# Nine-token loads, k^T v in array quarters, and weights staged in f32 and cast an expert ahead, in a fused linear-attention and top-1 MoE kernel

## The chip, the cores and the metric

The kernel runs on one core of a Trainium2 chip. The metric is device time in microseconds of one launch; three runs are taken, and their median counts. A profile of one execution by the hardware profiler is shown beside them.

## What is computed

Linear attention for 8 batches and 8 heads of 576 tokens and 64 dimensions, a root-mean-square norm of each head's output, and then a mixture of 8 experts that sends each of the 4608 tokens (512 wide, the 8 heads side by side) to one expert:

```python
kv = np.einsum('bhsd,bhse->bhde', k, v)
out = np.einsum('bhsd,bhde->bhse', q, kv)
rms = np.sqrt(np.mean(out * out, axis=-1, keepdims=True) + 1e-06)
x = (out / rms * g_norm)            # -> (4608, 512)
logits = x @ w_gate                 # (512, 8)
expert_idx = np.argmax(logits, axis=1)
gate_w = softmax(logits)[chosen]
for e in range(8):
    xe = x[expert_idx == e]
    ye = np.maximum(xe @ w1[e], 0.0) @ w2[e]   # w1 512 x 1024, w2 1024 x 512
    out[expert_idx == e] = gate_w * ye
```

All inputs and the output are f32. With the inputs of this case the experts get 564, 494, 600, 572, 539, 654, 585 and 600 tokens.

## The kernel before

The work has two stages. Every engine's instruction order is written out by hand.

**Attention, 36 slots.** Two batches make a group of nine slots; a slot is 128 tokens. `load_qkv` (L157) brings 512 tokens of all heads of one batch, four tokens a partition (runs of 1 KB), and `load_rem` (L164, DMAs at L167) the last 64 tokens of each head in 64-partition transfers with 256 B runs, the two batches of a group side by side. All of these go out on SP's queue; six `ld` buffers hold k, v and q of two batches, and the loads of batch b+2 are issued two slots ahead of batch b+1 (L415), so that they wait for buffers.

For each batch, `kv_mm` (L200, matmul L216) forms k^T v for one pair of heads: the two heads of the pair go to the two column halves of TensorE; four matmuls each have 128 rows, a fifth has 64. `kv_copy` (L221), `kv_t` (L227) and `kv_gate` (L235) put the result into `kvs`, 144 columns a head pair: 128 for the two heads on a block diagonal, 16 for the router's logits.

For each slot, `heads` (L192) has POOL copy the queries into contiguous form (L197), four slots at a time; `x_qt` (L251) transposes them on TensorE, `x_qs` (L263) copies the result on ScalarE, and `x_mm` (L267, matmul L278) multiplies with `kvs`: four matmuls, or eight of 64 weight columns in the ninth slot of a group. `x_norm` (L284) squares (ACT, L294), sums (DVE, L299), takes the inverse root on ACT (L303, L305) and scales (DVE, L307 and L311) into f16 rows `xg`.

After nine slots a `Route` (L318) finds each token's expert and its rank there, and `send` (L375) scatters the nine slots' rows into `xs_scratch` in device memory by nine indirect DMAs on POOL's queue (L386). Eight DMAs of zero rows (`blank`, L443) on SP's queue fill the rows below the capacity of 640 before anything is scattered. The lists `mid`, `late` and `last` hang the work of the next batches and the routes onto slots.

**FFN, nine jobs.** Experts 0 to 6, then a job "left" of up to 128 rows for what exceeds an expert's 640 rows, then expert 7. A job's rows come transposed by `fetch` (L562, DMA L567 on SP). `one` (L581) makes 320 columns of the first product in four matmuls (hp, L589), with the relu on ACT (L596); `two` (L600) makes 128 rows of the second (yp, L603), DVE scales by the gate weight (L608) and POOL scatters the rows to the output (L611). The left-over job gathers its rows by POOL (L544) and transposes them on TensorE (L630).

**Weights** (L119). w1 goes as f32 into one staging buffer on SP's queue (L125), and four casts with the norm's gain make the f16 copy (L132), by POOL for the first two experts and by DVE inside the FFN, two jobs ahead. w2 is cast in the DMA itself, on POOL's queue (L138). Each has three f16 buffers.

Of the kernel before, what the change touches and what calls it, by code (L numbers as in the profile page):

```python
# [28 lines left out]
def kernel(  # L29
# [16 lines left out]
    E = 8  # L46
# [3 lines left out]
    CAP = CT * 128  # L50
    NOV = (N - CAP) // 128
# [19 lines left out]
    o = 144 + CT  # L71
    for P in range(4):
        for bb in range(2):
            for j in range(4):
                c32[:, o + 9 * P + 4 * bb + j] = (2 * P + bb) * S + 4 * ar + j
        c32[:64, o + 9 * P + 8] = 2 * P * S + 512 + ar[:64]
        c32[64:, o + 9 * P + 8] = (2 * P + 1) * S + 512 + ar[:64]
# [40 lines left out]

    class Weights:  # L119
        def __init__(self, e):  # L120
            self.e = e if isinstance(e, bass.DynSlice) else slice(e, e + 1)

        def stage(self):
            self.st = P_w.tile([128, 4, F], F32, tag="wst", bufs=1, name="wst")
            nc.sync.dma_start(  # L125
                self.st, moe_w1[self.e, :, :].rearrange("o (t p) f -> p (o t) f", p=128)
            )

        def scale(self, eng, kk):
            if kk == 0:  # L130
                self.w1 = P_w.tile([128, 4, F], F16, tag="w1e", bufs=3, name="w1e")
            eng.tensor_scalar(  # L132
                self.w1[:, kk, :], self.st[:, kk, :], g2, 1.0, op0=ALU.mult, op1=ALU.mult
            )

        def second(self):
            self.w2 = P_w.tile([128, 8, D], F16, tag="w2e", bufs=3, name="w2e")
            nc.gpsimd.dma_start(  # L138
                self.w2, moe_w2[self.e, :, :].rearrange("o (t p) d -> p (o t) d", p=128)
            )  # L140
# [4 lines left out]
    W = [Weights(e) if e != "left" else None for e in order]  # L145

    with (
# [9 lines left out]
        def load_qkv(src, b):  # L157
            t = PA.tile([128, 8, 256], F32, tag="ld", bufs=6, name="ld")
            nc.sync.dma_start(
                t, src[b, :, 0:512, :].rearrange("h (p j) d -> p h (j d)", j=4)  # L160
            )
            return t

        def load_rem(src, b0, tag):  # L164
            t = PA.tile([128, 8, 64], F32, tag=tag, bufs=2, name=tag)
            for bb in range(2):
                nc.sync.dma_start(  # L167
                    t[64 * bb:64 * bb + 64, :, :],
                    src[b0 + bb, :, 512:576, :].transpose([1, 0, 2]),
                )  # L170
            return t

        ld, rem, qp, kvst = {}, {}, {}, {}

        def load_batch(b):
            ld["k", b] = load_qkv(k, b)
            ld["v", b] = load_qkv(v, b)
            if b % 2 == 0:
                rem["k", b // 2] = load_rem(k, b, "kr")
                rem["v", b // 2] = load_rem(v, b, "vr")  # L180
            if b == 0:
                nc.sync.dma_start(cf, c_f32.ap())
                nc.sync.dma_start(wg, moe_w_gate.rearrange("(t p) j -> p t j", p=128))
                nc.sync.dma_start(g2[0:64, :], g_norm.unsqueeze(1))
                nc.sync.dma_start(g2[64:128, :], g_norm.unsqueeze(1))
            ld["q", b] = load_qkv(q, b)
            if b % 2 == 0:
                rem["q", b // 2] = load_rem(q, b, "qr")
            if b == 0:
                nc.sync.dma_start(ch, c_f16.ap())  # L190

        def heads(b, j):  # L192

            if j == 0:
                qp[b] = PA.tile([128, 4, 8, 64], F32, tag="qp", bufs=2, name="qp")
            tv = ld["q", b].rearrange("p h (j d) -> p h j d", j=4)
            nc.gpsimd.tensor_copy(qp[b][:, j, :, :], tv[:, :, j, :])  # L197


        def kv_mm(b, i):  # L200
            if i == 0:
                kvst[b] = PSA.tile([128, 4, 64], F32, tag="kvp", bufs=1, name="kvp")
            kvp = kvst[b]
            kb, vb = ld["k", b], ld["v", b]
            kr, vr = rem["k", b // 2], rem["v", b // 2]
            r0 = 64 * (b % 2)
            for j in range(5):
                for hh in range(2):
                    h = 2 * i + hh
                    if j < 4:  # L210
                        lhs = kb[:, h, 64 * j:64 * j + 64]
                        rhs = vb[:, h, 64 * j:64 * j + 64]
                    else:
                        lhs = kr[r0:r0 + 64, h, :]
                        rhs = vr[r0:r0 + 64, h, :]
                    nc.tensor.matmul(  # L216
                        kvp[64 * hh:64 * hh + 64, i, :], lhs, rhs,
                        start=(j == 0), stop=(j == 4),
                    )

        def kv_copy(b):  # L221
            kvp, kvs = kvst[b], kvs_bufs[b % 4]
            for hh in range(2):
                ps = slice(64 * hh, 64 * hh + 64)
                nc.vector.tensor_copy(kvs[ps, :, 64 * hh:64 * hh + 64], kvp[ps, :, :])

        def kv_t(b):  # L227
            kvs = kvs_bufs[b % 4]
            kvtp = PSA.tile([128, 4, 128], F32, tag="misc", bufs=1, name="kvtp")
            for i in range(4):  # L230
                nc.tensor.transpose(kvtp[:, i, :], kvs[:, i, 0:128], ident)
            kvst[b] = PA.tile([128, 4, 128], F32, tag="kvt", bufs=1, name="kvt")
            nc.scalar.copy(kvst[b], kvtp)

        def kv_gate(b):  # L235
            kgp = PSA.tile([128, 4, 16], F32, tag="misc", bufs=1, name="kgp")
# [13 lines left out]

        def x_qt(s):  # L251
            P, r, b = split(s)
            if r < 8:
                j = r % 4
                src = qp[b][:, j, :, :]
            else:
                src = rem["q", P]
            qtp = PSA.tile([128, 4, 128], F32, tag="qtp", bufs=2, name="qtp")
            for i in range(4):
                nc.tensor.transpose(qtp[:, i, :], src[:, 2 * i:2 * i + 2, :], ident)  # L260
# [6 lines left out]
        def x_mm(s):  # L267
            P, r, b = split(s)
            if r < 8:
                parts = [(slice(0, 128), kvs_bufs[b % 4])]  # L270
            else:
                parts = [(slice(0, 64), kvs_bufs[(2 * P) % 4]),
                         (slice(64, 128), kvs_bufs[(2 * P + 1) % 4])]
            op = PSA.tile([128, 2, 512], F32, tag="op", bufs=2, name="op")
            for i in range(4):
                c0 = (i % 2) * 144
                for c, kvs in parts:
                    nc.tensor.matmul(  # L278
                        op[c, i // 2, c0:c0 + 144], qts[s][:, i, c], kvs[:, i, :],
                        start=True, stop=True,  # L280
                    )
# [36 lines left out]
        class Route:  # L318
# [28 lines left out]
            def ranks(self):  # L347

                G, oh = self.G, self.oh
                self.pp = PSA.tile([128, G, 8], F32, tag="misc", bufs=1, name="pp")  # L350
# [51 lines left out]
        for b in range(1, B):  # L402
            f = first_slot[b]
            n = 4 if b % 2 else 5
            plan = [[0, 1], [2, 3]] if n == 4 else [[0], [1, 2], [3]]
# [6 lines left out]
            for j in range(4):  # L412
# [322 lines left out]
```

## Time and profile before

| | |
|---|---|
| runs | 347.36 us median of 3 (342.71 to 352.43) |
| profiled execution | 340.94 us, of which the profile's span is 339.1 |
| attention | 0 to 177.35 us: PE busy 116.48, transfer share 0.89, 251 GB/s |
| FFN to the last yp | 177.35 to 332.80 us: PE busy 146.65, transfer share 0.89, 214 GB/s |
| tail | last rows scaled at 332.85, end of span 339.1 |
| busy in the span | PE 263.1, DVE 145.3, ACT 121.9, POOL 118.2 us |
| mean granted TensorE clock | 0.907 |

How to read it: the profile gives each engine's busy time, in total and in 40 slices of the span; the chain of waits follows the work that ended last back through whatever released it; the timeline lists the instructions of an engine in runs of equal ones, with the idle time before them in brackets and what ended it; windows give the same for chosen stretches, with the granted clock, the busy share of the 16 transfer engines and the rate. "issue" is time in which the profile shows nothing that an engine waited for. SPq and POOLq are the queues on which transfers are issued.

### The profile page before, as it was taken

The numbers are of one execution on the slowest core, as the hardware profiler recorded it, in microseconds if no ns is written. First come the engines' busy times: TensorE is split into PE (matmuls) and PEld (weight loads), VectorE is DVE, ScalarE is ACT, GpSimd is POOL, SyncE is SP. The second block draws the span as 40 slices with busy tenths as digits, with TensorE's granted clock in tenths as the row PEclk, the third lists the DMA queues.
The fourth block names the chain that finished last, engine by engine and source line by source line (L and its number), as shares of the span: only waits on it lengthen the run. The fifth ranks groups of instructions, "written<-read, shape, count | busy, mean of one in ns | idle before, by whom it ended". The sixth has DMA issues, their size and how long they took to land.

```text
span 339.1 us, 5512 instructions
## 1 busy us (share of the span) xinstructions
PE 263.1 (78%) x2119; PEld 187.4 (55%) x2119; DVE 145.3 (43%) x349; ACT 121.9 (36%) x295; POOL 118.2 (35%) x139
## 2 busy tenths in 40 slices
PE   0679499739986798753304999999999999779992
PEld 0578487628875677652202656464747474545650
DVE  0014516814674348578871253343340707054021
ACT  1024526234544354433201607070807070521620
POOL 4022020474117940758420052424250516225123
PEclk9999879987999599969555999999999999979998
DMA  7999999998699989547719978999999995999012
GB/s 237 222 324 305 269 274 350 244 359 286 190 279 342 367 272 226 130 100 151 278 48 181 292 204 154 279 172 265 287 221 327 175 346 158 270 256 223 24 53 95
DMA packets 84683, 78.30 MB, mean 231 GB/s; under 512 B 41771, under 2 KB 75819, under 8 KB 84656
## 3 DMA queue, kind: packets, MB, share of 16 engines
q1 hardware_dynamic: 70240, 54.29, 57.2%
q0 software_dynamic: 14416, 23.65, 30.0%
q8 instruction: 17, 0.28, 0.4%
q14 instruction: 10, 0.08, 0.1%
HBM read 66.46 MB, written 17.09 MB: 246 GB/s over the span
## 4 chain that ended last, share of the span: by engine, by line
PE 29%; DMA 24%; issue 20%; DVE 12%; POOL 6%; SPq 3%; ACT 3%; POOLq 1%; another core or an unknown queue 1%; DVEq 0%
DMA out_dram<-ys,idx 10%; PE op L278 9%; PE yp L603 5%; PE hp L589 5%; DMA xo<-xs_scratch,gi 4%; PE kvp L216 4%; POOL out_dram L611 4%; DMA ld<-in_v_dram 3%; DMA xs_scratch<-blank 3%; PE qtp L260 3%; SPq L167 2%; DMA ld<-in_q_dram 2%; DVE xg L311 2%; DVE dl L332 2%; PE kgp L238 1%
## 5 line engine op out<-in xcount | busy, mean ns | idle before, releaser
L596 ACT ACTIVATE ht<-hp 128x320 f16<-128x320 f32 (+1 forms) x136 | 57.9, 428 | 98.3 <-PE hp L589 62.6
L589 PE MATMUL hp<-xt,w1e 128*128 128x320 f16 (+1 forms) x544 | 76.9, 304 | 11.7 <-DMA xt<-xs_scratch 11.7
L611 POOL DMA_INDIRECT out_dram<-ys,idx x41 | 42.2, 1029 | 112.3 <-DVE ys L608 99.4
L589 PEld LDWEIGHTS <-w1e 128*128 128x128 f16 x544 | 53.3, 100 | 34.8 <-issue 11.8
L603 PE MATMUL yp<-w2e,ht 128*128 128x512 f16 x328 | 72.3, 379 | 0.0
L608 DVE TENSOR_SCALAR ys<-yp,mt 128x512 f32<-128x512 f32 x40 | 29.8, 750 | 91.6 <-PE yp L603 48.5
L278 PE MATMUL op<-kvs,qts 128*128 128x144 f32 (+1 forms) x320 | 51.3, 329 | 8.1 <-issue 5.2
L603 PEld LDWEIGHTS <-ht 128*128 128x128 f16 x328 | 32.1, 98 | 37.3
L386 POOL DMA_INDIRECT xs_scratch<-xg,sli x36 | 35.2, 979 | 50.0 <-DVE sli L384 39.4
L278 PEld LDWEIGHTS op<-kvs,qts 128*128 128x128 f32 (+1 forms) x320 | 43.2, 205 | 11.1 <-issue 6.0
L216 PE MATMUL kvp<-ld 128*64 128x64 f32 x512 | 25.3, 250 | 15.5 <-DMA ld<-in_v_dram 15.5
L197 POOL COPY qp<-ld 128x512 f32<-128x512 f32 x32 | 18.3, 614 | 53.3 <-DMA ld<-in_q_dram 53.2
L294 ACT ACTIVATE sq<-op 128x512 f32<-128x512 f32 x36 | 21.5, 597 | 41.3 <-PE op L278 30.2
L299 DVE TENSOR_REDUCE ms<-sq 128x8 f32<-128x512 f32 x36 | 24.5, 682 | 25.2 <-ACT sq L294 24.1
L265 ACT COPY qts<-qtp 128x512 f32<-128x512 f32 x36 | 21.0, 583 | 35.0 <-PE qtp L260 23.5
L216 PEld LDWEIGHTS kvp<-ld 128*64 128x64 f32 x512 | 20.6, 158 | 20.0 <-issue 19.0
L260 PE MATMUL qtp<-cf,qp 128*128 128x128 f32 x128 | 23.5, 315 | 8.8 <-issue 7.2
L311 DVE TENSOR_TENSOR xg<-op,rinv 128x512 f16<-128x512 f32 x36 | 24.5, 681 | 0.2
L260 PEld LDWEIGHTS qtp<-cf,qp 128*128 128x128 f32 x128 | 18.7, 169 | 9.5 <-issue 7.7
L132 DVE TENSOR_SCALAR w1e<-wst,g 128x1024 f16<-128x1024 f32 x28 | 21.0, 808 | 0.1
L307 DVE TENSOR_TENSOR lr<-op,rinv 128x64 f32<-128x64 f32 x36 | 8.1, 224 | 26.0 <-ACT rinv L305 19.4
L303 ACT ACTIVATE lnt<-ms,epsb 128x8 f32<-128x8 f32 x36 | 10.9, 302 | 11.0 <-DVE ms L299 8.9
(89 smaller groups left out, 143.5 us busy)
## 6 DMA issues: line engine op xcount, KB each, us to landing
wst<-in_moe_w_dram SPq DMA_DIRECT2D x9, 2048.0 KB
w2e<-in_moe_w_dram POOLq DMA_DIRECT2D x9, 1024.0 KB
ld<-in_k_dram SPq DMA_DIRECT2D x8, 1024.0 KB
ld<-in_v_dram SPq DMA_DIRECT2D x8, 1024.0 KB
ld<-in_q_dram SPq DMA_DIRECT2D x8, 1024.0 KB
xs_scratch<-blank SPq DMA_DIRECT2D x8, 193.5 KB
kr<-in_k_dram SPq DMA_DIRECT2D x8, 128.0 KB
vr<-in_v_dram SPq DMA_DIRECT2D x8, 128.0 KB
```

The costliest lines, as they stand in the source:

```text
L216: nc.tensor.matmul(kvp[64 * hh:64 * hh + 64, i, :], lhs, rhs, start=(j == 0), stop=(j == 4),)
L260: nc.tensor.transpose(qtp[:, i, :], src[:, 2 * i:2 * i + 2, :], ident)
L278: nc.tensor.matmul(op[c, i // 2, c0:c0 + 144], qts[s][:, i, c], kvs[:, i, :], start=True, stop=True,)
L294: nc.scalar.activation(sq.rearrange("p (c i h) n -> p c i (h n)", c=2, i=2), oc[:, :, :, 0:128], ACTF.Square,)
L299: nc.vector.reduce_sum(ms, sq, axis=AXX)
L311: nc.vector.tensor_tensor(xg[:, r, 0:512].rearrange("p (c i h n) -> p c i h n", c=2, i=2, h=2), ox, _bc(r4, 4, 64), op=ALU.mult,)
L386: nc.gpsimd.indirect_dma_start(out=xs_views[9 * self.P + g0 + t], out_offset=IndirectOffsetOnAxis(ap=sli[:, t:t + 1], axis=0), in_=xgs[sel ...
L589: nc.tensor.matmul(hp, self.w.w1[:, kk, f * 128:(f + 1) * 128], self.xt[:, kk, ws * wd:(ws + 1) * wd], start=(kk == 0), stop=(kk == 3),)
L596: nc.scalar.activation(self.ht[:, f, ws * wd:(ws + 1) * wd], hp, ACTF.Relu)
L603: nc.tensor.matmul(yp, self.ht[:, f, t * 128:(t + 1) * 128], self.w.w2[:, f, :], start=(f == 0), stop=(f == 7),)
L608: nc.vector.tensor_scalar(ys, yp, self.mt[:, t, 1:2].bitcast(F32), None, op0=ALU.mult)
L611: nc.gpsimd.indirect_dma_start(out=self.views[t], out_offset=IndirectOffsetOnAxis(ap=self.idx[:, t:t + 1], axis=0), in_=ys, in_offset=None ...
```

## The change

- **Loads.** k, v and q of a batch come in one form: 9 tokens of a head a partition, two heads on the 128 partitions, four head pairs along the row (runs of 2304 B). The remainder loads go. k and v have six buffers, q three of its own; the first batch's k and v come in two pieces each. The constants and the zero rows are issued by ACT.
- **k^T v.** A head's tokens now lie on one half of the partitions. For two head pairs, nine steps of four 64x64 matmuls: row half by head of the pair, column half by pair, accumulated apart for the two row halves.
- **Queries.** `x_qp` copies them slot by slot on POOL, four slots ahead. Every slot is two tokens of 64 partitions, and `x_mm` has eight matmuls of 64 weight columns in every slot. kvtp, kgp, pp and cp share the two PSUM buffers of qtp.
- **Capacity** 608 instead of 640: hp is 304 columns wide, the last of five yp tiles has 96 rows.
- **Weights.** Both are loaded as f32 on SP's queue into five staging buffers. w1 comes in four DMAs of 64 partitions (its rows ordered as x is now laid out), and is cast by DVE (POOL for the first expert), one expert ahead; w2 is cast by four ACT copies, one expert ahead. Two f16 buffers each. Expert 0's w1 and w2 and expert 1's w1 are loaded during attention.

```diff
-    CAP = CT * 128
+    CAP = 608
+    WIDTHS = [128, 128, 128, 128, 96]
...
-        def stage(self):
-            self.st = P_w.tile([128, 4, F], F32, tag="wst", bufs=1, name="wst")
+        def load1(self, buf):
+            self.s1 = buf.rearrange("p (t f) -> p t f", t=4)
+            view = moe_w1[self.e, :, :].rearrange("o (c i h p) f -> (o i) p c h f", c=2, i=2, h=2)
+            for i in range(2):
+                ps = slice(64 * i, 64 * i + 64)
+                for c in range(2):
+                    nc.sync.dma_start(self.s1[ps, 2 * c:2 * c + 2, :], view[i, :, c, :, :])
+
+        def load2(self, buf):
+            self.s2 = buf.rearrange("p (t d) -> p t d", t=8)
             nc.sync.dma_start(
-                self.st, moe_w1[self.e, :, :].rearrange("o (t p) f -> p (o t) f", p=128)
+                self.s2, moe_w2[self.e, :, :].rearrange("o (t p) d -> p (o t) d", p=128)
             )
...
-        def second(self):
-            self.w2 = P_w.tile([128, 8, D], F16, tag="w2e", bufs=3, name="w2e")
-            nc.gpsimd.dma_start(
-                self.w2, moe_w2[self.e, :, :].rearrange("o (t p) d -> p (o t) d", p=128)
-            )
+        def cast2(self, kk):
+            nc.scalar.copy(self.w2[:, 2 * kk:2 * kk + 2, :], self.s2[:, 2 * kk:2 * kk + 2, :])
...
-        def load_qkv(src, b):
-            t = PA.tile([128, 8, 256], F32, tag="ld", bufs=6, name="ld")
-            nc.sync.dma_start(
-                t, src[b, :, 0:512, :].rearrange("h (p j) d -> p h (j d)", j=4)
+        def load(name, b, parts=1):
+            src = {"k": k, "v": v, "q": q}[name]
+            tag, bufs = ("lq", 3) if name == "q" else ("lkv", 6)
+            ld[name, b] = PA.tile([128, 4, 9 * Dh], F32, tag=tag, bufs=bufs, name=tag)
+            view = src[b].rearrange("(i hh) (p j) d -> (hh p) i (j d)", hh=2, j=9)
...
+            for j in range(9):
+                js = slice(Dh * j, Dh * j + Dh)
                 for hh in range(2):
+                    rs = slice(64 * hh, 64 * hh + 64)
+                    for ipar in range(2):
+                        i = 2 * ip + ipar
+                        nc.tensor.matmul(
+                            kvp[64 * ipar:64 * ipar + 64, hh, Dh * ip:Dh * ip + Dh],
+                            kb[rs, i, js], vb[rs, i, js],
+                            start=(j == 0), stop=(j == 8),
+                        )
...
+        def x_qp(s):
+            P, r, b = split(s)
+            qps[s] = PA.tile([128, 2, 4, 64], F32, tag="qp", bufs=4, name="qp")
+            if r < 8:
+                tv = ld["q", b].rearrange("p i (j d) -> p j i d", j=9)
+                nc.gpsimd.tensor_copy(qps[s], tv[:, 2 * (r % 4):2 * (r % 4) + 2, :, :])
...
+            for ip in range(2):
+                for hh in range(2):
+                    for tok in range(2):
+                        kvs = kvs_bufs[(b if r < 8 else 2 * P + tok) % 4]
+                        nc.tensor.matmul(
+                            op[64 * tok:64 * tok + 64, ip, 144 * hh:144 * hh + 144],
+                            qts[s][:, 2 * tok + ip, 64 * hh:64 * hh + 64],
+                            kvs[:, 2 * ip + hh, :],
+                            start=True, stop=True,
+                        )
...
-            nc.sync.dma_start(
-                xs.ap()[e * N + CAP - 192:e * N + CAP, :].rearrange("(p r) c -> p (r c)", r=2),
+            nc.scalar.dma_start(
+                xs.ap()[e * N + CAP - 160:e * N + CAP + 32, :].rearrange("(p r) c -> p (r c)", r=2),
                 blank,
             )
...
+            if s + 4 < 36:
+                x_qp(s + 4)
...
             jobs[0].fetch()
-            W[1].second()
+            for kk in range(4):
+                W[0].cast2(kk)
+            load_next(1, 2)
             jobs[1].fetch()
-            W[2].second()
+            load_next(2, 1)
+            load_next(2, 2)
             jobs[0].place()
...
                         job.one(ws, f)
+                        if ws == 0 and f % 2 == 1 and n + 1 < len(order):
+                            W[n + 1].cast1(nc.vector, f // 2)
+                            if f == 7:
+                                load_next(n + 3, 1)
...
                     job.two(t)
+                    if nxt is not None and t < 4:
+                        W[n + 1].cast2(t)
+                if nxt is not None:
+                    for t in range(job.nt, 4):
+                        W[n + 1].cast2(t)
+                    load_next(n + 3, 2)
```

`load_next(n, which)` loads w1 or w2 of job n into the next of the five staging buffers in turn.

## Prediction

> **What bounds the kernel now.** I read the page first, then the chain of waits, then PE's timeline and the windows around each gap. On the page, part 2:
>
> ```profile
> PE   0679499739986798753304999999999999779992
> ...
> PEclk9999879987999599969555999999999999979998
> DMA  7999999998699989547719978999999995999012
> ...
> q1 hardware_dynamic: 70240, 54.29, 57.2%
> q0 software_dynamic: 14416, 23.65, 30.0%
> ```
>
> One slice is 8.5 us. There are two stages: attention with holes in PE (slices 1-21, to 177.35 us), and the FFN (177.35 to 332.85), where PE is full but for one dip near 290. The transfer engines are at 0.9 almost everywhere; they go quiet only after 312. So this kernel has two limits close together. The chain of waits says where PE has to wait:
>
> ```profile
> 11.78 6.38 DMA ld<-in_q_dram
> 18.21 1.15 POOL qp L197 x2
> 19.36 11.07 DMA xs_scratch<-blank
> ...
> 30.94 11.84 DMA ld<-in_v_dram
> ...
> 71.60 5.23 issue
> ...
> 284.39 14.11 DMA xo<-xs_scratch,gi
> ```
>
> The first query tile lands at 18.16. SP sits on the zero rows (L443) until 30 and issues the loads of batch 2 after them, so PE stands at slot 5. At 71.60 (5.23), 110.02 (2.49) and 143.41 (4.66) PE waits for a query copy (L197) that stands on POOL behind nine scatters (L386; 64.93-76.2 in the first burst). At 284.39 the gather of the single left-over tile queues behind a weight load. PE's timeline prices two of these:
>
> ```profile
> 42.91 1.12 PE L216 MATMUL kvp<-ld 128*64 128x64 f32 x16 [5.05 <-DMA ld<-in_v_dram]
> ...
> 298.55 0.40 PE L630 MATMUL xp<-ch,xo 128*128 128x128 f16 x4 [3.82 <-DMA xo<-xs_scratch,gi]
> 298.78 4.55 PE L589 MATMUL hp<-xt,w1e 128*128 128x320 f16 x20
> ```
>
> The windows (engine columns, granted clock, transfer share, GB/s) give rates of single transfers:
>
> ```profile
> 9.50:10.50 1.00, 0.05 (x2) 0.08 (x3) 0.00 (x0) 0.00 (x0) 0.00 (x0) 1.00 1.33 212
> 192.00:194.00 2.00, 2.00 (x15) 1.27 (x14) 0.00 (x0) 1.64 (x4) 0.00 (x0) 1.00 1.03 418
> ```
>
> 212 GB/s: the remainder loads, 256 B runs onto 64 partitions. 418: w1, 4 KB runs onto 128 partitions. The 1 KB q/k/v loads ran at 340 (5.00 to 7.50).
>
> **Attention, part by part.** *Start and loads.* Zero rows and constants leave SP for ACT's queue; the remainder loads go. The bytes ahead of the first query are 2.36 MB of k and v and 1.18 of q, 3.54 in all, with the zero rows (1.55) now beside them. At 0.34-0.375 MB/us, with 1.5 us to issue, q lands near 16 instead of 18.16: slot 0 at about 21.5 instead of 23.73. Batch 2 is then loaded without the 11 us of zero rows ahead of it. Between slots 5 and 10 the old starts were 44.42 to 61.98; unstalled slots last 2.5 us without k^T v, 2.9-3.35 with it and 4.95 for routing. Laying ten such slots from 21.5 puts slot 10 at 52.4: -9.6 in all.
>
> *Query copies.* One per slot, four ahead, instead of four per batch. By the issue order of the changed kernel, x_qp(14), (23) and (32) are queued on POOL behind a burst of nine scatters (11.3 us, e.g. 64.93 to 76.2). Slots 10 to 13 have their copies, so PE has four slots (some 11-12 us) of work, and at the later bursts also k^T v of the next batch. Set against the burst, the wait is longer than the one before by 0.6, 1.5 and 2.3: +4.4. If the four slots hide it, 0.
>
> *k^T v in quarters.* Per batch 72 matmuls in 64x64 quarters (144 records) take the place of 40 (80 records):
>
> ```profile
> L216 PE MATMUL kvp<-ld 128*64 128x64 f32 x512 | 25.3, 250 | 15.5 <-DMA ld<-in_v_dram 15.5
> ...
> L216 PE MATMUL kvp<-vr,kr 64*64 64x64 f32 x128 | 11.6, 262 | 0.8 <-DMA vr<-in_v_dram 0.8
> ```
>
> In the timeline two records on different column halves start 7 ns apart and such pairs follow each other every 58 ns; a move between 128 and 64 rows costs 0.15 us; ten pairs and two moves are the 0.87 us of one head pair, 1.75 for two. If all four quarters run together, two head pairs are 18 steps of 58 ns, 1.04, with moves 1.3: -0.9 a batch. If the row halves go one after another, 36 steps, 2.1 and moves, 2.35: +1.2 a batch. I take the first, since the column halves do run together here; no row shows two row halves at once, so both ends stay. Six batches after slot 5 lie on PE's path only in part, since some slots wait for POOL: -1.8.
>
> *Output matmuls* in 64 weight columns: 16 such records took 1.13-1.20 (slots 8), eight full ones 1.18-1.25. Nothing. The shared score buffers (kvtp, kgp, pp and cp in two buffers with the query transposes) can add a wait; hidden behind DVE's routing, bound 0 to +2.
>
> Attention: -9.6 + 4.4 - 1.8 = -7. With row halves one after another, the lead at slot 10 is 7.5 and 4.8 us come on later (not all of 6 x 1.2): -7.5 + 4.4 + 4.8 = +2.
>
> **FFN.** *608 rows.* hp is 64 matmuls in 8.66; at 304 of 320 columns 8.23: -0.43 by eight jobs, -3.4. The last yp tile has 96 rows but the same 512 columns: nothing. Only one expert overflows by either capacity, so there is one left-over job before and after.
>
> *Left-over gather.* w2 no longer goes through POOL's queue, so the 14.11 us gather shrinks, and with it PE's 3.82 and the cold matmuls behind it (20 in 4.55 where 20 x 0.135 = 2.7): -5.6. If it stays late, 0. With xt0 landing 6 us in (5 now; W1's load is ahead of it), 2.4 of cold clock in job 0 (11.15 against 8.7), 8.23 + 8.64 = 16.87 a job and 4.8 for the left-over one (PE 3.84 now, and its relus behind a copy on ACT), the FFN alone is 6 + 2.4 + 8 x 16.87 + 4.8 = 148.2, against 155.5.
>
> *Casts.* DVE keeps four 128x1024 casts per job (0.81 each), and ACT gets four of w2. ACT's rows are 438 ns for 320 columns and about 590 for 512, which gives 1.0 us for 1024: 4 a job, beside 16 x 0.43 = 7 of relu in 16.9. Hidden, if the weights are there; if not, relu stands behind the copy on ACT and the next hp with it.
>
> *The weights themselves.* Seven w1 and eight w2 now fall in the FFN (six and six before). A w2 load is 2.10 MB of 2 KB runs: 5.5 us at 390. It took 6.8 with the cast. w1 is now four transfers onto 64 partitions each. Low end: 2.10 MB at 400-418 is 5.2. High end: at the 212 of the only 64-partition row, 9.9. That row has small runs, and 256 B transposes onto all 128 partitions ran at 288, so run length explains part of it. I take 9.8, since nothing else onto 64 partitions is in the trace.
>
> The Trainium skill speaks against this edit too: "SBUF — State Buffer", section "Door 1: The DMA port swizzle (why [64,N] ≈ [32,N])", has a transfer onto partitions 0-63 reach half of the ports, 196 GB/s at 1 MiB against 328 onto all, and a second transfer onto the other half add 6%. The row's 212 agrees. By the page's figures a w1 load would be some 9.6-10.7 us (an estimate) and the whole as forecast here or a little over; were the rule not to hold for queued halves, the whole would be rival A.
>
> Now SP's queue, counted from the fetch of xt0. That is through at 4. Then come eight w2 (44), seven w1 (68.6) and seven transposes of 2.4 (16.8; 0.6 MB at the 288 GB/s above and a start). The outputs, on the other queue, are 1.25 MB a job, 3.0 us at 418; of five jobs' outputs I let 0.45 come on top (7), since the two queues together kept the share at 0.96 while PE hardly stood. With 2 us to land, xt8, the last, is there at 142. PE is through job 7 at 131.3, stands 11, is cold again (+2.4) and needs 16.87: 161.5. Outputs wholly hidden but for 0.2 give 157.7, not hidden at all 169.7. So +2 to +14, and I take +6.5. Until job 7 nothing is late by this count: five staging buffers let the loads run two experts ahead of the casts, and what is late at the end is late because job 7 lasts 4.8 us while its expert's weights are as large as any.
>
> **Sum.** -7 + 6.5 = -0.5 on a profiled execution of 340.94 (span 339.1 and 1.84 around it). The median shown is 347.36, 6.4 above that run. Against the median: 347.
>
> **Rivals.**
> *A, w1 at full rate.* The 64-partition halves overlap. For it: transfers of one queue run into each other in this trace. Against it: 212. FFN 148.2-150, so -5.5 to -7.3, sum about -14: 333.
> *B, slower: the row halves of k^T v go one after another.* Place: PE in attention. It decides once a two-pair group lasts longer than 1.75; at 2.35, +2 and +6.5: 356. Should each move between halves cost the 0.15 seen between 128 and 64 rows, 18 moves make 2.7 more per group and the result passes 366. For it: no row shows two row halves together. Against it: the columns' 7 ns.
> *C, slower: the FFN is bound by transfers more deeply.* 2304 B runs, transposes at 3.2 or outputs wholly in the way: FFN 170 instead of 161.5, 356. Against it: before, at a share of 0.89 to 0.96, PE hardly stood.
> *D, the copies still come too late:* x_qp behind the scatters, that the change does not take away. It is in the sum at +4.4; hidden it would be 343.
>
> **How the numbers follow.** Quarters together 0.7, w1 at half rate 0.7, C in a third of the latter. Likeliest case 0.32 at 347 (own range 341 to 354); A 0.20; B 0.21; C 0.17; A with B, at 342, 0.10 (D spreads within each). The range goes from 331, the lower part of A, to 364, above B and C; what passes 366 is left out. A measurement of this kernel can tell about 2% from no change: faster 0.27 (A and the edge of the likeliest), same 0.35, slower 0.38.
>
> **What would show it.** Right: q landing near 16; slot 10 near 52; two k^T v pairs within 1.4 us; w1's packets at about twice 160-172 ns for 4 KB, or windows near 210 GB/s while w1 alone loads; a stall of some 11 us ahead of the last expert, released by xt or w2. Wrong: w1 windows above 350 and no stall in the FFN (A); groups of 36 matmuls above 1.75 (B); PE standing at every expert, not only at the last (C). A wait nowhere listed, on ACT or the shared score buffers, would make the whole sum wrong.

## The result, and the profile after

392.32 us (median of 4, 389.42 to 393.70) against 345.03 (median of 4, 339.94 to 352.43): 1.148 times as long, 95% interval 1.135 to 1.162. The profiled execution took 393.7 with a span of 391.8. (The kernel before was run once more beside it, so its median is no longer the 347.36 of three runs.) Cut at the first transposed fetch and at the end of the last yp, the two profiles differ in every stage:

| us | before | after | difference |
|---|---|---|---|
| attention, to the fetch of xt0 | 177.35 | 194.08 | +16.7 |
| FFN, to the end of the last yp | 155.5 | 186.7 | +31.2 |
| from there to the end of the span | 6.3 | 11.0 | +4.7 |

The forecast for the three rows was -7, +6.5 and nothing.

The page of the changed kernel, its rows of 40 slices (9.8 us each) and its queues:

```profile
PE   2297977397738684472069999698697939931980
...
PEclk9998989879968698576569999989899978995895
DMA  7999992389229902018399999999999999997020
...
q1 hardware_dynamic: 52208, 71.09, 64.7%
q0 software_dynamic: 4928, 14.25, 10.1%
q10 hardware_dynamic: 1920, 1.81, 1.5%
q8 instruction: 23, 0.38, 0.4%
```

The transfer row, which was near 9 almost throughout before, is now full at the start, more than half empty in the second half of attention (2, 0, 1), and then at 9 without a break for all of the FFN, where PE has dips (6, 8, 6, 7, 3, 3). So in its second half attention waits for something that is no data transfer, and the FFN for transfers. PE's timeline shows a stop of each kind:

```profile
20.24 1.11 PE L251 MATMUL qtp<-cf,qp 128*128 128x128 f32 x4 [5.16 <-POOL qp L241]
...
124.96 1.27 PE L195 MATMUL kvp<-lkv 64*64 64x64 f32 x71
131.25 0.36 PE L195 MATMUL kvp<-lkv 64*64 64x64 f32 x1 [5.02 <-issue]
...
253.66 3.57 PE L608 MATMUL yp<-w2b,ht 128*96 128x512 f16 x8 [3.82 <-DVE ys L613]
...
331.22 0.39 PE L635 MATMUL xp<-ch,xo 128*128 128x128 f16 x4
...
358.86 0.41 PE L593 MATMUL hp<-xt,w1b 128*128 128x304 f16 x1 [10.56 <-DMA xt<-xs_scratch]
```

The left-over gather (331.22) no longer stops PE. Batch 2's v no longer stops slot 5. In their place: 71 of the 72 records of one k^T v group run, and the last comes 5 us later, with nothing that the profile names ("issue"); and the fifth yp of a job waits for DVE, whose `ys` are the scaled rows. DVE itself waits for `mt`, the token numbers and gate weights of the next job's rows, which are loaded behind those rows; `place` turns these numbers into the addresses of the output scatter. What DVE waits for, by total, times and longest:

```profile
DVE raw L580 <- DMA mt<-xs_scratch: 60.7, 8, 10.3
DVE ys L613 <- DMA out_dram<-ys,idx: 49.8, 8, 8.2
```

The k^T v group, by its form, and two windows inside job 2 (the columns are those of the prediction's windows: engines, granted clock, transfer share, GB/s), one while w1 loads and one while w2 loads with outputs beside it:

```profile
L195 PE MATMUL kvp<-lkv 64*64 64x64 f32 x1152 | 23.6, 233 | 20.2 <-DMA lkv<-in_v_dram 10.7 <-issue 9.6
```

```profile
234.00:238.00 4.00, 4.00 (x32) 2.88 (x30) 0.69 (x2) 2.32 (x6) 2.96 (x3) 1.00 1.03 212
242.00:246.00 4.00, 4.00 (x23) 2.05 (x21) 3.23 (x5) 1.20 (x3) 2.21 (x1) 1.00 1.03 406
```

Of the 20.2 us that PE stood ahead of k^T v, 9.6 have no releaser. Both windows have all 16 transfer engines busy; w1 gets 212 GB/s, w2 406. The 4 KB packets of w1 took 315 ns in the median, where they took 172 before. (q10 is ScalarE's queue, with the constants and zero rows; q8 brings PE its instructions.)

### The profile page after: what moved, and what is told of

The parts are those of the page before. It is cut to its first block, busy times and chain, and to the rows that moved or that the text cites. A ratio compares the mean times of both kernels' runs of the same rounds, so it can differ in the third digit from the quotient of the medians.

```text
span 391.8 us, 7170 instructions
## 1 busy us (share of the span) xinstructions
PE 269.3 (69%) x2887; PEld 187.7 (48%) x2887; DVE 144.2 (37%) x353; ACT 155.3 (40%) x331; POOL 117.2 (30%) x133
## 4 chain that ended last, share of the span: by engine, by line
issue 26%; DMA 14%; PE 12%; POOL 9%; DVE 6%; ACT 2%; POOLq 1%; SPq 0%; DVEq 0%
DMA out_dram<-ys,idx 13%; POOL out_dram L616 8%; PE op L267 5%; PE hp L593 3%; PE qtp L251 2%; ACT w2b L149 1%; DMA xt<-xs_scratch 1%; PE kvp L195 1%; DVE dl L323 1%; POOL xs_scratch L377 1%; DVE xg L302 1%; DVE lg L317 1%; PE kgp L221 1%; ACT qts L258 0%; PE kvtp L214 0%
## 5 line engine op out<-in xcount | busy, mean ns | idle before, releaser
L593 PE MATMUL hp<-xt,w1b 128*128 128x304 f16 (+1 forms) x544 | 74.5, 299 | 25.8 <-DMA xt<-xs_scratch 22.2
L608 PE MATMUL yp<-w2b,ht 128*128 128x512 f16 (+1 forms) x328 | 77.8, 397 | 18.0 <-DVE ys L613 18.0
L600 ACT ACTIVATE ht<-hp 128x304 f16<-128x304 f32 (+1 forms) x136 | 55.1, 414 | 57.3 <-PE hp L593 37.4
L593 PEld LDWEIGHTS <-w1b 128*128 128x128 f16 x544 | 53.7, 101 | 47.2 <-issue 14.8
L608 PEld LDWEIGHTS <-ht 128*128 128x128 f16 (+1 forms) x328 | 35.2, 108 | 56.6 <-issue 23.0
L267 PE MATMUL op<-kvs,qts 128*64 128x144 f32 x576 | 54.0, 341 | 3.6 <-issue 2.1
L613 DVE TENSOR_SCALAR ys<-yp,mt 128x512 f32<-128x512 f32 (+1 forms) x40 | 28.6, 746 | 71.7 <-DMA out_dram<-ys,idx 49.8
L149 ACT CAST w2b<-stg 128x1024 f16<-128x1024 f32 x36 | 35.2, 1042 | 44.1 <-DMA stg<-in_moe_w_dram 44.1
L267 PEld LDWEIGHTS op<-kvs,qts 128*64 128x64 f32 x576 | 42.2, 164 | 9.7 <-issue 4.2
L285 ACT ACTIVATE sq<-op 128x512 f32<-128x512 f32 x36 | 21.5, 597 | 60.3 <-PE op L267 41.3
L195 PE MATMUL kvp<-lkv 64*64 64x64 f32 x1152 | 23.6, 233 | 20.2 <-DMA lkv<-in_v_dram 10.7
L290 DVE TENSOR_REDUCE ms<-sq 128x8 f32<-128x512 f32 x36 | 24.6, 682 | 21.5 <-ACT sq L285 18.7
L195 PEld LDWEIGHTS kvp<-lkv 64*64 64x64 f32 x1152 | 20.8, 146 | 23.4 <-issue 19.1
```

The source lines that it names most:

```text
L149: nc.scalar.copy(self.w2[:, 2 * kk:2 * kk + 2, :], self.s2[:, 2 * kk:2 * kk + 2, :])
L195: nc.tensor.matmul(kvp[64 * ipar:64 * ipar + 64, hh, Dh * ip:Dh * ip + Dh], kb[rs, i, js], vb[rs, i, js], start=(j == 0), stop=(j == 8),)
L267: nc.tensor.matmul(op[64 * tok:64 * tok + 64, ip, 144 * hh:144 * hh + 144], qts[s][:, 2 * tok + ip, 64 * hh:64 * hh + 64], kvs[:, 2 * ip + ...
L290: nc.vector.reduce_sum(ms, sq, axis=AXX)
L593: nc.tensor.matmul(hp, self.w.w1[:, kk, f * 128:(f + 1) * 128], self.xt[:, kk, ws * wd:(ws + 1) * wd], start=(kk == 0), stop=(kk == 3),)
L600: nc.scalar.activation(self.ht[:, f, ws * wd:(ws + 1) * wd], hp, ACTF.Relu)
```

## The experiments

They ran in three sets on two chips on which the kernel before takes 337 to 339 us; the changed kernel was run again with the third set and took 391.2 (first row). "Start of FFN" is the first hp, "FFN" from there to the end of the last yp, both from the profile. Each median is of three runs.

| | median | start of FFN | FFN |
|---|---|---|---|
| after_again: the changed kernel | 391.2 | 196.9 | 181.7 |
| a_w1_full | 361.5 | 191.8 | 158.0 |
| c_place_late | 383.4 | 195.5 | 175.0 |
| e_less_code | 376.1 | 182.6 | 182.0 |
| k_wide | 387.7 | 192.7 | 182.0 |
| f_start | 383.5 | 187.7 | 182.7 |
| i_split_send | 371.2 | 176.5 | 183.5 |
| h_full_less | 349.8 | 178.8 | 157.6 |
| m_best | 342.3 | 173.2 | 156.2 |
| the kernel before (its first profile) | 337-339 | 182.3 | 150.5 |
| b_w1_half | 354.1 | 186.7 | 162.3 |
| d_more_code | 339.0 | 181.4 | 152.2 |
| n_before_split | 320.6 | 162.1 | 150.5 |

> The changed kernel once more, on the chip of the other runs (where the kernel before takes 337-339 us, not 345), so that they have it beside them: by its ratio of 1.148, 386 to 389 us.

It took 391.22 (387.19 to 391.57), 1.157 times the kernel before (1.144 to 1.169), 2 us above the expectation.

### The FFN: the w1 loads

```diff
 a_w1_full
-                for c in range(2):
-                    nc.sync.dma_start(self.s1[ps, 2 * c:2 * c + 2, :], view[i, :, c, :, :])
+            nc.sync.dma_start(
+                self.s1, moe_w1[self.e, :, :].rearrange("o (t p) f -> p (o t) f", p=128)
+            )
...
-                    xg[:, r, 0:512].rearrange("p (c i h n) -> p c i h n", c=2, i=2, h=2),
-                    ox, _bc(r4, 4, 64), op=ALU.mult,
...
+                for c in range(2):
+                    nc.vector.tensor_tensor(
+                        xg[:, r, 256 * c:256 * c + 256].rearrange("p (h i n) -> p i h n", i=2, h=2),
+                        ox[:, c], _bc(r4[:, c], 3, 64), op=ALU.mult,
+                    )
 b_w1_half: in the kernel before, w1 by the four transfers of the changed kernel
 c_place_late: nxt.place() moved from the third hp group to behind the five yp tiles
```

> The changed kernel with w1 loaded by one transfer onto all 128 partitions; so that this is possible xg is written in head order, in two DVE instructions a slot instead of one (36 more on DVE, some 10 us of DVE time spread over attention, at most 5 us on the path). Theory T, the FFN is bound by the transfer queue because a w1 load takes 10.6 us onto 64 partitions at a time: a 4 KB packet falls from 315 ns to 160-175, a w1 load to about 5.5, the cycle of one expert on the queue from 22.7 to about 18; the FFN (186.6 us from the first transposed fetch to the last yp) falls by 20 to 30, the whole from 392 to 362-373. Rival O, the order of the instructions (DVE's place waits for mt behind the weights and holds every ys): the loads get shorter but PE still stands at each fifth yp; FFN above 178, the whole 383 or more.

> The kernel before with only its w1 loads turned into four transfers of 64 partitions each (same bytes, same 4 KB runs, other row order: the rows of w1 are assigned to other partitions, so the products are not those of the reference). Theory T: 4 KB packets go from 160-175 ns to about 315, a w1 load from 5.5 to about 10; the transfer share of the FFN was 0.89 to 0.96, so nearly all of six loads times 4.8, less the 0.05 to 0.1 that was free, comes on: +10 to +25 on the FFN of 155.5, the whole 355 to 372 against 345. Rival, the half rate is hidden in a queue that is two experts ahead: within 2%.

> The changed kernel with the next job's place (raw and idx on DVE, which wait for mt) moved behind this job's five yp tiles. Theory T: PE no longer stands at the fifth yp but in front of the next hp, for as long; the whole stays within 2% of 392. Rival O: the 18.0 us that PE stood at yp behind DVE are saved and the cold matmuls after them: 370 to 378.

a: 361.5, inside the range of theory T. The w1 packets fell to 159 ns, the FFN from 181.7 to 158.0. PE's waits at yp behind DVE fell from 19.4 us to 3.4 (first line the changed kernel run again, the others a; in a the 8.2 stand at the last expert):

```profile
PE yp L608 <- DVE ys L613: 19.4, 4, 7.1
```

```profile
PE hp L592 <- DMA xt<-xs_scratch: 8.2, 1, 8.2
...
PE yp L607 <- DVE ys L612: 3.4, 2, 1.9
```

Another 5.1 us came ahead of the FFN, of which 3.2 are one stop of PE beside the first w1 load (4.99 us before, 1.84 in a).

b: 354.1 (350.88 to 357.00 against 333.45 to 339.57), +15.5 on the kernel before by the medians, at the near end of the range; by the profiles 11.8 in the FFN and 4.4 ahead of it. (Other than the expectation says, each row of w1 goes to the same partition as before; nothing else is changed.) Its 4 KB packets took 272 ns in the median, not the 315 of the changed kernel. Seen from both sides, the four transfers cost some 12 us of FFN in the kernel before and 24 in the changed one.

c: 383.4, 2.0% less than the changed kernel run again and 2.2% below the 392 of the expectation, just past what theory T allowed and far from rival O's 370 to 378. PE stood at no yp any more, and in front of five hp instead (the 11.5 is the start of the FFN, as in every run):

```profile
PE hp L593 <- DMA xt<-xs_scratch: 29.4, 5, 11.5
```

So the order of DVE's work (place of the next job holds the ys of this one) costs some 7 us of the FFN (181.7 to 175.0), and the half-rate w1 loads 24 (a).

### Attention: how densely PE's instructions come

PE's instructions arrive in 16 KB packets on queue q8, 17 before and 23 after. In the trace after, the packets that start at 32.01, 48.66, 88.11 and 128.40 each have PE standing around them, inside or behind a k^T v group. In all four PE goes on 1.4 to 1.5 us after the packet has ended. The four stops also stand at fixed counts of PE's instructions (matmuls, weight loads and semaphore instructions of the trace): ahead of number 705, 1217, 2241 and 3265, in the run again as well, which are 512, 1024 and 1024 apart. The 23 packets cover the trace's 5853 instructions at some 256 a packet, so these are the places where one packet ends and the next is needed.

```diff
 e_less_code
-                qts[s][:, 2 * tok + ip, 64 * hh:64 * hh + 64]     (two matmuls of 64 weight columns)
+                qts[s][:, 2 * ip + hh, :]                         (one of 128, in slots with r < 8;
+                                                                   the ACT copy writes qts in that order)
 d_more_code, in the kernel before
-                op[c, i // 2, c0:c0 + 144], qts[s][:, i, c], kvs[:, i, :]
+                op[c, i // 2, c0 + 72 * w:c0 + 72 * w + 72], qts[s][:, i, c], kvs[:, i, 72 * w:72 * w + 72]
+                (for w in range(2), and c in two halves of 64 in every slot)
 k_wide, in the changed kernel
-                kb[rs, i, js], vb[rs, i, js]
+                kb[rs, i, js], _bc(vb[rs, i, js], 1, 2)           (128 output columns, the second 64 unread)
```

> The changed kernel with the output matmuls of the first eight slots of a group joined to four of 128 weight columns (the ScalarE copy of the transposed queries writes them side by side): 128 matmuls, 256 records and as many weight loads fewer on PE, with the same time on PE (16 records of 64 columns took 1.20, eight of 128 took 1.18-1.25). Theory L, PE stands in attention because its instructions are loaded too late (16 KB loads every 256 instructions, 15 of them before 148 us, with 2.0-2.2 us of standing right behind five of them and 5.0 behind one): two loads fewer, attention ends 3 to 6 us earlier, the whole 386-390. Rival, those stops are waits for buffers that the profile does not name: unchanged, 390-394.

> The kernel before with each output matmul of 128 weight columns and 144 output columns split into four (two halves of the weight columns, two of the output columns): 768 more records and as many weight loads on PE, as many as the change brought, with nothing else changed. Theory L (PE runs out of loaded instructions when many short ones follow each other): some six more 16 KB loads of instructions before 150 us, stops of about 2 us behind several of them, attention 8 to 15 us longer, the whole about 350 against 339. Rival, only PE's own time counts: the eight records of a slot took 1.18-1.25 and 32 short ones take about as long, within 2% of the kernel before; if 32 take longer (each record 60 ns or more), PE's busy time tells it, 0.7 us a slot.

e: 376.1, a gain of 15 where theory L had 3 to 6 and its rival none. The profile has unnamed stops of 1.8 us at k^T v groups where the changed kernel, run again, has 9.4:

```profile
PE kvp L195 <- issue: 9.4, 3, 5.0
```

```profile
PE kvp L195 <- issue: 1.8, 2, 1.6
```

One of 1.9 at the output matmuls went too, and one of 2.5 at a transpose is new, so 7 us are the stops themselves. Behind three of the four stops of the changed kernel the granted clock is 0.5 for 3.4 us (a group of 16 output records takes 1.82 to 2.19 us there instead of 1.20); from the first output record behind the stop to the gate's matmuls 4.75 to 4.89 us pass, and 3.29 behind the fourth, where the clock stays: 4.6 in all. What is left of the 15 no row here takes apart.

d: 339.0 (333.06 to 341.69 against 335.29 to 339.44), no change. As many records as the change brought cost nothing in the kernel before, and PE has no unnamed stop:

```profile
L279 PE MATMUL op<-kvs,qts 128*64 128x72 f32 x1152 | 51.8, 247 | 0.4 <-DVE xg L312 0.4
```

Theory L as written was wrong: the number alone does not matter. In d the densest group is 64 instructions (32 matmul records and 32 weight loads) in 1.27 us, 50 a microsecond; in the changed kernel a k^T v group is 144 in 1.28, 112 a microsecond. That gave theory L2.

> The changed kernel with every k^T v matmul streaming its v columns twice (128 output columns, half of them a copy that nothing reads): the same number of instructions, but a group of 72 records should last about 2.4 us instead of 1.28. Theory L2 (768 more records in the output matmuls cost nothing, so it is not their number but how densely they come: 144 instructions in 1.28 us outrun the loading of instructions, 50 a microsecond do not): the stops inside and behind k^T v groups (9.6 us at kvp, 2.1 at op, 4-9 elsewhere in attention) go away or shrink below 3 us together, which pays for most of the 16 groups x 1.1 us; the whole within 2% of the changed kernel. Rival (the stops have nothing to do with the rate of instructions): they stay where they are and the longer groups come on top, +12 to +18.

k: 387.7. The same place in the changed kernel (first two lines) and in k_wide:

```profile
47.77 1.26 PE L195 MATMUL kvp<-lkv 64*64 64x64 f32 x67
51.32 0.34 PE L195 MATMUL kvp<-lkv 64*64 64x64 f32 x5 [2.29 <-issue]
```

```profile
46.73 2.18 PE L195 MATMUL kvp<-lkv 64*64 64x128 f32 x67
49.20 0.44 PE L195 MATMUL kvp<-lkv 64*64 64x128 f32 x5 [0.29 <-issue]
```

The groups last 2.20 instead of 1.28 us, 16 times, and the kernel is not slower: the 2.29 became 0.29, a 2.12 became 0.45, a 1.91 vanished, and 4.99 became 3.01, 3.8 together at the k^T v groups where 9.4 stood (below 3 was expected). This is what L2 expects of the rate, and its rival (+12 to +18) is out. The stop of 5 us lies beside the first half-rate w1 load (121 to 131 us), behind which the instruction packet started only at 128.40; in a_w1_full no stop at k^T v is over 2.2.

The traces say more closely which rate counts: that over the 256 instructions ahead of the place where a packet ends. In the changed kernel run again they passed in 3.5 us ahead of each of the four stops; at its other such places in attention they took 5.3 us or more, and PE did not stand. In k_wide the same four took 4.8 to 4.9, and 0.5 us or less is left of two stops and nothing of a third. In d no 256 instructions in a row take less than 5.3 us, in the kernel before none less than 9.1. This also explains e, whose k^T v groups are as dense as those of the changed kernel: with fewer instructions between the groups the packets end elsewhere, and only one place has 3.5 us ahead of it (the stop of 1.6).

The other half is when the next packet comes. With the transfer engines full (share 1.04 to 1.06) it began 3.0 to 3.4 us into the 256 instructions ahead of three of the four stops, and 5.95 us into them beside the w1 load, the stop of 5 us. Where the engines were nearly idle (share 0.05 to 0.07) it began 0.6 to 0.8 us into them. In f one place has 3.5 us ahead of it and no stop; its packet began 1.0 us in. In e the stop of 2.5 has 8.4 us ahead of it; its packet began 8.3 us in. So in these runs PE stands where many short instructions meet full transfer engines.

### The start, the bursts, and all together

```diff
 f_start: first loads ahead of the constants in program order; zero rows two a slot in slots 1 to 4
 i_split_send
             at(last, s + 1, rt.send)
+            if G == 9:
+                for m in range(3):
+                    at(last, s + 1 + m, rt.rows, range(3 * m, 3 * m + 3))
 h_full_less = a_w1_full + e_less_code
 m_best = h + f + i + c, and xt of the last job fetched before its weights
 n_before_split: the kernel before + i, and its zero rows on ScalarE's queue in slots 1 to 4
```

> The changed kernel with the constants issued behind the first loads of k, v and q in program order (so that SP's fourth load no longer waits until a constant has landed; it stood until 8.10 us) and the zero rows issued two a slot in slots 1 to 4 instead of at 7-14 us beside the first loads. If the start was mis-sized by these two: q lands near 14-16 instead of 19.5, slot 0 starts near 19-21 instead of 25.1. Theory T2 (transfers run at 370-390 GB/s without a gap until slot 10, so what is saved at the start comes back later): slot 10 no more than 2 us earlier. Rival (a gap of the start is a gap of the whole): the whole 4 to 6 us less than the changed kernel.

f: 383.5, -7.7 where the rival of T2 had 4 to 6. Slot 0 starts at 21.84 instead of 25.18, slot 10 at 54.18 instead of 62.97 (first two lines the changed kernel run again, the others f):

```profile
25.18 2.19 PE L267 MATMUL op<-kvs,qts 128*64 128x144 f32 x16 [0.32 <-DVE kvs L224]
...
62.97 1.20 PE L267 MATMUL op<-kvs,qts 128*64 128x144 f32 x16
```

```profile
21.84 2.19 PE L267 MATMUL op<-kvs,qts 128*64 128x144 f32 x16 [0.32 <-DVE kvs L224]
...
54.18 1.20 PE L267 MATMUL op<-kvs,qts 128*64 128x144 f32 x16
```

The gap of the start was a gap of the whole, and theory T2 was wrong. Of the 8.8 us at slot 10, 3.3 stand there at slot 0 already; between the two slots, instruction stops of 1.91 and 2.29 us have become one of 0.73. In the run again SP's fourth load goes out at 8.71 and batch 1's k at 14.13, in f at 7.20 and 8.89; the zero rows, whose packets ran from 8 to 22 us beside the first loads, come later. f changes the constants and the zero rows together and does not tell the two apart.

> The changed kernel with each burst of nine row scatters spread over three slots, three a slot, so that the query copies stand behind three scatters (3.8 us) and not nine (11.4). If the copies behind the burst are what PE stands for (23 us in four waits), each of three bursts gives back 4 to 6 us: the whole 12 to 16 us less than the changed kernel, 373 to 377. Rival: the scatters themselves, which rows are late for, or DVE and ScalarE standing beside them, bound these slots: less than 5 us.

i: 371.2, -20 where 12 to 16 were expected. PE's waits for the query copies fell from 23.3 to 12.0 (first line the changed kernel run again, second line i):

```profile
PE qtp L251 <- POOL qp L241: 23.3, 4, 6.6
```

```profile
PE qtp L251 <- POOL qp L241: 12.0, 5, 3.8
```

The unnamed stops at k^T v groups fell from 9.4 to 6.7 as well; the remaining 6 or so no row here takes apart.

> The changed kernel with both edits of the runs before: w1 on all 128 partitions and four output matmuls a slot. If the two causes lie in different stages and add, -27 and -12: 348 to 352 where the kernel before has 339. If code loading and the w1 loads hinder each other only together (the 5.0 us stop of PE stood beside the first w1 load), less than the sum, 353 to 357.

h: 349.8, -41.4 where the two alone gave -29.7 and -15.1: two causes in two stages, and they add but for 3.4 us. Some 3.2 of that is probably the long stop beside the first w1 load, which each of the two edits shortens by itself.

> The changed kernel with w1 on 128 partitions, four output matmuls a slot, scatters three a slot, constants and zero rows behind the first loads, place behind the yps, and the rows of the last expert fetched ahead of its weights: if all add, 388 less 27, 12, 16, 4 to 8 and 3 to 8, that is 318 to 327, below the kernel before (338). If the start and the bursts give back the same waits, 328 to 335.

m: 342.3 (336.82 to 346.03), not the 318 to 335 expected, and not below the kernel before. Start, bursts and instruction stops give back the same waits: attention ends at 173.2, only 3 ahead of i alone. In the FFN one stop is left, at the last expert:

```profile
303.91 0.43 PE L616 MATMUL hp<-xt,w1b 128*128 128x304 f16 x1 [4.91 <-DVE w1b L142]
...
312.68 8.03 PE L616 MATMUL hp<-xt,w1b 128*128 128x304 f16 x48 [3.30 <-ACT ht L623]
```

Its weights are cast during the job before it, as for every expert; but that job is the left-over one and lasts 4 us.

> The kernel before with two of these edits alone: scatters three a slot, and the zero rows issued on ScalarE's queue in slots 1 to 4. The waits of PE for a query copy (about 15-22 us in four) shrink by 8 to 12, the 8 us at slot 5 (v of batch 2 behind the zero rows) by 5 to 8, if the FFN starts as much earlier: 319 to 326.

n: 320.6 (315.5 to 323.3), inside the range, the fastest of all and 17 below the kernel before. PE's wait for query copies is 1.0 us in all, and its FFN starts 20 us earlier and is as long as before:

```profile
PE qtp L260 <- POOL qp L197: 1.0, 1, 1.0
```

Nothing of the change is in it but that ScalarE issues the zero rows. How much of the 17 each of its two edits gives was not run.

## Why the prediction was wrong, step by step

- **w1 at half rate: right.** 9.8 was forecast for a load and 10.6 measured (from its first packet at 230.26 to w2's first at 240.82), 212 GB/s. The rule of the Trainium skill, "SBUF — State Buffer", section "Door 1: The DMA port swizzle (why [64,N] ≈ [32,N])", holds here, also for four queued transfers of alternating halves. Rival A is out.
- **The sum of the queue: the step that failed most** (+6.5 forecast, +31 measured). An expert was given 9.8 + 5.5 + 2.4 + 1.35 = 19.1 us. In the trace one takes 22.7 (w1's first packet at 230.26, the next expert's at 252.98): w1 10.6, w2 with the outputs 8.3, transpose, mt and the gap ahead of w1 3.8. The outputs were not half hidden: the four scatters issued from 233.0 to 237.9 us move their first packet at 239.91, as w1 ends, and come on top of w2. That was rival C, priced at 170 for the FFN, which took 186.7. Even that was low, since the shortage was taken to show at the last expert only. There it came as forecast (11 forecast, 10.56 behind xt). But it showed from job 2 on as well, at DVE, with 18.0 us of waits at yp: place waits for mt, mt is loaded behind the transposed rows, and the ys of a finished job stand behind place. The sum followed the queue into PE and not into DVE. (A slip beside it: the 161.5 that the sum gives is 6.0 above 155.5, not 6.5.)
- **The start: loads that go out later than counted** (-2.2 at slot 0, -9.6 at slot 10; measured +1.4 and +0.9). The sum counts the bytes, with the zero rows among them, and has them flow without a break after 1.5 us: only with the zero rows' 1.55 MB does its rate put q near 16. In the trace SP's fourth load goes out at 8.10, the loads' packets pause from 7.89 to 9.11, and q lands at 19.5. Between slots 0 and 10 the two instruction stops of the next item come on top (2.12 and 2.23). In f the query copies start at 16.33, slot 0 at 21.84 (21.5 forecast) and slot 10 at 54.18 (52.4 forecast), so the size of the gain was right and the change as made did not give it.
- **k^T v in quarters: the group right, the consequence missed.** 1.3 us was forecast for two pairs, 1.28 came; rival B is out. But "nothing" for the output matmuls and a gain for the quarters were counts of PE's busy time only. The term left out, put at nothing, is the loading of PE's instructions: 9.4 us of stops at these groups, some 2 us at the output matmuls, and the matmuls behind them at a granted clock of 0.5; e gave back 15. In the profile of before no line shows it; what could have told it is that the change raises the instructions of two head pairs from 80 in 1.75 us to 144 in 1.3.
- **Query copies behind the bursts: right in kind, and in the sum.** +4.4 forecast (0.6, 1.5 and 2.3). Slots 12 to 14 took 12.2 us instead of 13.3, slots 21 to 24 as long as before (16.3), slots 30 to 32 15.8 instead of 9.9: +4.9 in all, but from the third burst alone, so that the sum agrees in part by luck. (In the first profile a part of these waits stands ahead of the gate's matmuls, 9.1 us without a name.)
- **608 rows and the left-over gather: right.** hp 8.43 instead of 8.86 in the timeline, no wait at the gather.
- **The tail: not in the sum.** +4.7. The last scatter starts 2.0 us after its ys instead of 0.9, and between the last packet and the end of the span lie 5.8 us instead of 2.3. POOL's last drain stands there, 7.60 us long instead of 3.97. That second part is in a_w1_full and m_best too and not in b, d or n, so it belongs to something that the changed kernel has and these have not. No run here took it apart, and its cause stays open.

The range ended at 364, because each rival was priced alone. The runs show C, the start and a term that was not listed at all, together.

## What to carry to other kernels

Count a transfer queue with everything that goes over it, at the rates of the shapes it will have, and follow the last thing on it through every engine that waits for it in order: the price is paid at the first such place, not at the last. A layout that makes one load whole (q, k and v in one form) can split another (w1 onto halves of the partitions), and the split one here was the larger. When a change makes many short matmuls of few long ones, compare instructions per microsecond over some hundreds in a row, not only busy time.

## What the runs showed of the hardware

- PE stood some 2 us where it needed the next 16 KB packet of its instructions, had passed the 256 ahead of that place in 3.5 us, and the packet had begun 3.0 to 3.4 us into them. In each of the four stops of the changed kernel it went on 1.4 to 1.5 us after the packet's end. The Trainium skill, "Runtime: NRT & Kernel Launch", section "Instruction fetch mechanics", calls the cost of crossing such a block mostly hidden; it is in d, and is not in the changed kernel.
- A scatter on POOL that meets DVE's four f32 casts takes 3.17 us instead of 0.98, five times in the changed kernel, and none in c, where the two do not meet. The Trainium skill, "SBUF — State Buffer", in its box on DVE blocking a software DMA, has POOL unable to write a transfer's descriptors while DVE runs an operation that takes both ports; its example is an f32 copy, here it is a scaling from f32 to f16. The scatter, in the trace after:

```profile
222.32 3.17 POOL L616 DMA_INDIRECT out_dram<-ys,idx  x1 [4.27 <-DVE ys L613]
```

- The transfer share reads 1.03 at 212 GB/s as it does at 406. Only read beside the rate does a full share tell how much the engines carry. In the changed kernel the scatters of a job that were issued while such a w1 load ran moved only when it was all but over (issued from 212.5, moved from 219.4; issued from 233.0, moved from 239.9).
